# Order of the four products per chunk, and x times v in two halves, in an FFT convolution with an expert layer behind it

## The chip, the cores and the metric

The kernel runs on one core of a Trainium2 chip. The metric is the device time of one execution in microseconds; the time before is a median of three runs. Engines are named as in the profile: PE (TensorE), DVE (VectorE), ACT (ScalarE), POOL (GpSimd), SP (the queue that issues every DMA here).

## The reference

```python
u = x * v                                  # (4, 12480, 128)
L = 2 * S
Uf = np.fft.rfft(u, n=L, axis=1)
Hf = np.fft.rfft(h_filt, n=L, axis=0)      # h_filt: a small MLP of pos_emb, times exp(-0.01 t)
y = np.fft.irfft(Uf * Hf[None], n=L, axis=1)[:, :S, :]
x = x * y                                  # (49920, 128)
h = x @ w_in                               # 2048 wide
out = (h * clip(h + 3, 0, 6) / 6) @ w_out
```

A long convolution of u = x times v with a filter, done by Fourier transforms, gates x; an expert layer with two matrix products follows.

## The kernel before, in words

The transform of length 64 x 196 is split in two stages forth and two stages back, each a set of matrix products with constant tables. The work comes in eight groups of channels. The function `filter` makes the filter's spectrum and the first stage of group 0. Then `period(g)` runs for g = 0 to 7, each with 25 chunks of four of the 99 frequencies. In one period TensorE does, for each chunk, the second stage of group g (L301, `spectra`, for the chunk after the one in hand) and the third stage (L546, `third_stage`, for a chunk three back). In between stand the transposes of group g - 1 (L557, `back`) with its fourth stage (L575), and, in eight visits of each period but the last, the first stage of group g + 1 (L282, `visit`). The output of the convolution goes to device memory. `last_turn` ends the convolution, and the class `Moe` then does the expert layer.

A chunk's way over the engines is this. TensorE puts the second stage into a PSUM bank `s2`, of which there are two. ACT copies it with real and imaginary half exchanged into the bank `sw`, of which there is one: two instructions, L499 and L500 (`swapped`). DVE then makes four products with the filter's spectrum `h`. Two read `s2`: `pq` at L520 and `pa` at L521. Two read `sw`: `pq2` at L522 and `pa2` at L523. POOL adds them up at L527 in three steps: `pq` into half of `pa`, `pq2` into half of `pa2`, and `pa2` into `pa`. (In period 0 the third step of two chunks in three is done by DVE at L533, behind the next chunk's products.) The third stage reads `pa`. L521 is the last reader of `s2`, and L523 the last reader of `sw`; the next second stage but one needs the first, and the next swap the second.

There is no scheduler: each engine takes its instructions in the order in which the functions are called, and waits for the semaphores of what it depends on. In an iteration the call of `chunk` comes first (products, third stage, second stage of the next chunk), then `fourth_stage`, `gate_next`, and then a loop with `back`, `weight` and `visit`. Two or three light chunks follow each other, about 2.5 us of TensorE each, and then a chunk with a visit and a fourth stage, about 8 us; this is called a cycle here.

`gate_next` multiplies x and v for sixteen channels of one piece (L453, on POOL) into a tile `u`, in the chunks of the lists GATES (`1, 4, 8, 11, 14, 17, 20, 22`) and GATES0 (for period 0). Behind it `load_next` issues four DMAs on SP for a later x and v (L442). Each product is made two halves ahead of the visit that reads it. In periods 1 to 6, `weight` puts steps of decoding the expert layer's weights on DVE (L225 to L247), three per call in some chunks, behind the chunk's products; period 7 has no visits.

Of the kernel before, what the change touches and what calls it, by code (L numbers as in the profile page):

```python
# [13 lines left out]
ALU = mybir.AluOpType  # L14
# [23 lines left out]
G = 32  # L38
GB = 2
# [149 lines left out]
def pool(tc, name, bufs=1, **kw):  # L189
    return tc.tile_pool(name=name, bufs=bufs, reuse_waits="tile", **kw)  # L190
# [60 lines left out]
class Conv:  # L251
    def __init__(self, tc, nc, left, right, x, v, c_tab, d_tab, g_tab, ident, hd, yd, weights):
        self.tc, self.nc, self.left, self.right = tc, nc, left, right
        self.x, self.v, self.g_tab, self.ident, self.hd, self.yd = x, v, g_tab, ident, hd, yd
        self.c_tab, self.d_tab, self.weights = c_tab, d_tab, weights
        self.loaded, self.gated, self.n_loaded = [], [], 0
        self.first, self.second, self.pend, self.steps = [], [], [], None
        self.tabs, self.n_tabs, self.hs, self.n_hs = [], 0, [], 0
        self.out, self.sum = None, None
        self.keep = right.enter_context(pool(tc, "keep", side="right"))  # L260
        self.z = [self.keep.tile([128, K2, COLS], F32, name=f"z{i}") for i in range(2)]
        self.dtab = self.keep.tile([K2, 2, 64], F32, name="dtab")
        big = left.enter_context(pool(tc, "big"))
        self.ctab = big.tile([R[0], 2 * K2], F32, name="ctab")
# [181 lines left out]
    def gate_next(self):  # L446

        if self.loaded:
            half, xt, vt, again = self.loaded.pop(0)
            if half == 0:  # L450
                self.gated.append(self.up.tile([R[0], G, N1], F32, tag="u", name="u"))
            u = self.gated[-1][:, half * G // 2 : (half + 1) * G // 2, :]
            self.nc.gpsimd.tensor_tensor(out=u, in0=xt, in1=vt, op=ALU.mult)  # L453
            if again:
                self.load_next()
# [47 lines left out]
    def products(self, item):  # L503

        nc, P = self.nc, 128
        g, c, kw, t, tab = item
        sw = self.swapped(t, kw)
        hs = self.hs.pop(0)
        a = self.pr.tile([P, CH, 2 * GB, G], F32, tag="a", name="pa", bufs=4)
        a2 = self.pr.tile([P, CH, 2 * GB, G], F32, tag="a2", name="pa2")  # L510
        q = self.pr.tile([P, CH, GB, G], F32, tag="q", name="pq")
        q2 = self.pr.tile([P, CH, GB, G], F32, tag="q2", name="pq2")
        uv = t.rearrange("p (k s g) -> p k s g", k=CH, g=G)[:, :kw]
        sv = sw.rearrange("p (k s g) -> p k s g", k=CH, g=G)[:, :kw]

        def h(ci, si, m):
            return hs[:, ci, :kw, si, :].unsqueeze(2).to_broadcast([P, kw, m, G])

        mul, add = ALU.mult, ALU.add
        nc.vector.tensor_tensor(out=q[:, :kw], in0=uv[:, :, :GB], in1=h(0, 1, GB), op=mul)  # L520
        nc.vector.tensor_tensor(out=a[:, :kw], in0=uv, in1=h(0, 0, 2 * GB), op=mul)  # L521
        nc.vector.tensor_tensor(out=q2[:, :kw], in0=sv[:, :, :GB], in1=h(1, 1, GB), op=mul)  # L522
        nc.vector.tensor_tensor(out=a2[:, :kw], in0=sv, in1=h(1, 0, 2 * GB), op=mul)  # L523
        self.load_h()

        def plus(x, y):
            nc.gpsimd.tensor_tensor(out=x, in0=x, in1=y, op=add)  # L527

        plus(a[:, :kw, GB:], q[:, :kw])
        plus(a2[:, :kw, GB:], q2[:, :kw])  # L530
        if self.sum:
            s, s2 = self.sum
            nc.vector.tensor_tensor(out=s, in0=s, in1=s2, op=add)  # L533
        self.sum = None
        if g == 0 and c % 3:
            self.sum = a[:, :kw], a2[:, :kw]
        else:
            plus(a[:, :kw], a2[:, :kw])
        return g, c, kw, tab, a
# [61 lines left out]
    def period(self, g):  # L601


        n = 0
        if g == 1:
            self.ext.close()
            self.dp = self.left.enter_context(pool(self.tc, "dp"))
            self.wp = self.right.enter_context(pool(self.tc, "wp", 2, side="right"))
        for c in range(NCHUNK):
            end = min(32, 32 * (c + 1 - START) // (NCHUNK - 1 - START))  # L610
            self.chunk(g, c)
            if c in (0, NCHUNK - 1):
                self.fourth_stage()
            if c in (GATES if g else GATES0):
                self.gate_next()
            while n < end:
                if g:
                    self.back(g - 1, 4 * n)
                    self.weight(n)
                n += 1  # L620
                if n % VISIT == 0:
                    if g + 1 < NG:
                        self.visit(g + 1, n // VISIT - 1)
                    if n < 28 and g + 1 < NG:
                        self.fourth_stage()
                if n % VISIT == 2 and VISIT < n < 28 and g + 1 == NG:
                    self.fourth_stage()
# [267 lines left out]
```

## Time and profile before

| | us |
|---|---|
| median of 3 runs (3169.38 to 3170.16) | 3170.02 |
| the profiled execution | 3166.51 |
| its span | 3164.7 |
| filter and first stage of group 0 | about 160 |
| period 0 | about 85 |
| periods 1 to 6, each | 107 to 111 |
| period 7, and the last turn | about 87, and 53 |
| expert layer | about 2120 |

A row of the timeline gives the start and length in us, the engine, the line, the operation, the output and inputs by name, the shape, how many instructions were merged, and in brackets the engine's idle time before it with what ended it by the profile. The bank `s2` and the bank of the third stage both appear as `s`. A second or third stage of one chunk is eight TensorE records (six in the last chunk). A row of the waits gives who waited for whom, the total in us, how often, and the longest wait.

### The profile page before, as it was taken

The numbers are of one execution on the slowest core, as the hardware profiler recorded it, in microseconds if no ns is written. First come the engines' busy times: TensorE is split into PE (matmuls) and PEld (weight loads), VectorE is DVE, ScalarE is ACT, GpSimd is POOL, SyncE is SP. The second block draws the span as 40 slices with busy tenths as digits, with TensorE's granted clock in tenths as the row PEclk, the third lists the DMA queues.
The fourth block names the chain that finished last, engine by engine and source line by source line (L and its number), as shares of the span: only waits on it lengthen the run. The fifth ranks groups of instructions, "written<-read, shape, count | busy, mean of one in ns | idle before, by whom it ended". The sixth has DMA issues, their size and how long they took to land.

```text
span 3164.7 us, 53332 instructions
## 1 busy us (share of the span) xinstructions
PE 3114.2 (98%) x19916; PEld 2633.9 (83%) x19916; DVE 2305.8 (73%) x2707; ACT 2351.7 (74%) x3039; POOL 2079.2 (66%) x1240
## 2 busy tenths in 40 slices
PE   9989999999999999999999999999999999999999
PEld 8978888888887788888888888888888888888887
DVE  4467666767654777777777777777777777777776
ACT  2367767767766777878787777777777877777777
POOL 1188777777874666666666666666666666666666
PEclk9999999999999999999999999999999999999999
DMA  6688888787855111111111110111111111111110
GB/s 236 211 205 230 228 230 234 218 238 221 228 172 202 54 36 35 38 42 35 35 40 31 41 41 30 41 39 32 41 36 35 39 32 41 38 33 40 40 31 24
DMA packets 232273, 304.66 MB, mean 96 GB/s; under 512 B 38055, under 2 KB 159310, under 8 KB 231118
## 3 DMA queue, kind: packets, MB, share of 16 engines
q1 hardware_dynamic: 232014, 301.26, 32.6%
q8 instruction: 157, 2.57, 0.3%
q14 instruction: 102, 0.84, 0.1%
HBM read 224.87 MB, written 76.28 MB: 95 GB/s over the span
## 4 chain that ended last, share of the span: by engine, by line
PE 68%; POOL 0%; DVE 0%; ACT 0%; DMA 0%; issue 0%; ACTq 0%
PE acc L827 11%; PE acc L823 11%; PE acc L824 11%; PE ph L788 11%; PE ph L790 11%; PE ph L789 11%; PE ts L575 0%; PE s L557 0%; PE ts L557 0%; POOL pa L527 0%; DMA yd<-y 0%; POOL glo L812 0%; DVE y L596 0%; ACT o L594 0%; ACT ghi L810 0%
## 5 line engine op out<-in xcount | busy, mean ns | idle before, releaser
L812 POOL TENSOR_TENSOR glo<-g,ghi 128x1024 fp32r<-128x1024 f32 x588 | 1404.4, 2397 | 761.2 <-ACT ghi L810 761.0
L800 DVE SCALAR_TENSOR_TENSOR g<-r,ph 128x1024 f32<-128x1024 f32 (+1 forms) x784 | 949.7, 1211 | 408.7 <-ACT r L798 408.3
L798 ACT ACTIVATE r<-ph,three 128x1024 f32<-128x1024 f32 (+1 forms) x784 | 871.1, 1111 | 273.6 <-PE ph L790 273.4
L810 ACT CAST ghi<-g 128x1024 fp32r<-128x1024 f32 (+1 forms) x784 | 811.1, 1035 | 1.9 <-DVE g L800 1.0
L788 PE MATMUL ph<-xhi,win_hi 128*128 128x512 f32 (+1 forms) x1568 | 608.5, 388 | 0.0
L789 PE MATMUL ph<-xlo,win_hi 128*128 128x512 f32 (+1 forms) x1568 | 608.4, 388 | 0.0
L790 PE MATMUL ph<-xhi,win_lo 128*128 128x512 f32 (+1 forms) x1568 | 608.3, 388 | 0.0
L824 PE MATMUL acc<-ghi,wout_lo 128*128 128x512 f32 (+1 forms) x1568 | 608.0, 388 | 0.0
L823 PE MATMUL acc<-ghi,wout_hi 128*128 128x512 f32 (+1 forms) x1568 | 607.9, 388 | 0.0
L827 PE MATMUL acc<-glo,wout_hi 128*128 128x512 f32 (+1 forms) x1568 | 481.3, 388 | 0.6 <-POOL glo L812 0.6
L527 POOL TENSOR_TENSOR pa<-pa,pq 128x256 f32<-128x256 f32 (+1 forms) x400 | 295.6, 747 | 171.3 <-DVE pa L521 133.2
L788 PEld LDWEIGHTS ph<-xhi,win_hi 128*128 128x128 f32 x1568 | 294.4, 188 | 61.5 <-issue 0.8
L827 PEld LDWEIGHTS acc<-glo,wout_hi 128*128 128x128 f32 x1568 | 293.6, 188 | 61.7 <-POOL glo L812 1.5
L824 PEld LDWEIGHTS acc<-ghi,wout_lo 128*128 128x128 f32 x1568 | 294.5, 188 | 60.5
L790 PEld LDWEIGHTS ph<-xhi,win_lo 128*128 128x128 f32 x1568 | 294.4, 188 | 60.5
L823 PEld LDWEIGHTS acc<-ghi,wout_hi 128*128 128x128 f32 x1568 | 294.4, 188 | 60.4
L789 PEld LDWEIGHTS ph<-xlo,win_hi 128*128 128x128 f32 x1568 | 294.5, 188 | 60.4
L812 DVE TENSOR_TENSOR glo<-g,ghi 128x1024 fp32r<-128x1024 f32 x196 | 283.7, 1448 | 0.0
L520 DVE TENSOR_TENSOR pq<-s,h 128x256 f32<-128x256 f32 (+1 forms) x200 | 84.1, 421 | 255.7 <-POOL pa L527 162.2
L761 DVE TENSOR_TENSOR xy<-xt,yt 128x512 f32<-128x512 f32 x96 | 258.7, 2695 | 0.0
L301 PE MATMUL s<-z,tab 128*128 128x128 f32 x1584 | 213.9, 278 | 35.5 <-DVE pa L521 27.9
L527 POOL TENSOR_TENSOR pa<-pa,pa 128x512 f32<-128x512 f32 (+1 forms) x184 | 232.5, 1263 | 14.4
(61 smaller groups left out, 3620.6 us busy)
## 6 DMA issues: line engine op xcount, KB each, us to landing
tab<-in_g_tab SPq DMA_DIRECT2D x192, 256.0 KB
h<-hd SPq DMA_DIRECT2D x384, 128.0 KB
yd<-y SPq DMA_DIRECT2D x64, 512.0 KB
xt<-in_xt SPq DMA_DIRECT2D x98, 256.0 KB
out<-o SPq DMA_DIRECT2D x97, 256.0 KB
xt<-in_x SPq DMA_DIRECT2D x64, 384.0 KB
vt<-in_v SPq DMA_DIRECT2D x64, 384.0 KB
yt<-yd SPq DMA_DIRECT2D x256, 64.0 KB
```

The lines of the kernel that those rows point to most:

```text
L527: nc.gpsimd.tensor_tensor(out=x, in0=x, in1=y, op=add)
L761: self.nc.vector.tensor_tensor(out=xy.rearrange("p (n e c) -> p n e c", e=4, c=GH), in0=xt.rearrange("p (n e c) -> p n e c", e=4, c=GH), i ...
L788: nc.tensor.matmul(ph[:, i, :ne], self.win_hi[:, sl], hi[:, :ne], start=True, stop=False)
L789: nc.tensor.matmul(ph[:, i, :ne], self.win_hi[:, sl], lo[:, :ne], start=False, stop=False)
L790: nc.tensor.matmul(ph[:, i, :ne], self.win_lo[:, sl], hi[:, :ne], start=False, stop=True)
L798: nc.scalar.activation(r[:, :, :ne], ph[:, :, :ne], AF.Relu, bias=self.three)
L800: nc.vector.scalar_tensor_tensor(out=g[:, :, :ne], in0=r[:, :, :ne], scalar=6.0, in1=ph[:, :, :ne], op0=ALU.min, op1=ALU.mult)
L810: nc.scalar.copy(ghi[:, :, :ne], g[:, :, :ne])
L812: e.tensor_tensor(out=glo[:, :, :ne], in0=g[:, :, :ne], in1=ghi[:, :, :ne].bitcast(F32), op=ALU.subtract)
L823: nc.tensor.matmul(a, self.wout_hi[:, f, :], ghi[:, i, :ne], start=(f == 0), stop=False)
L824: nc.tensor.matmul(a, self.wout_lo[:, f, :], ghi[:, i, :ne], start=False, stop=False)
L827: nc.tensor.matmul(a, self.wout_hi[:, f, :], glo[:, i, :ne], start=False, stop=(f == NFC - 1))
```

## The change

Three things are changed. In `products` the two products that read `sw` come before the two that read `s2`, and POOL's first two additions change places in the same way. `gate_next` makes only eight of the sixteen channels; the other eight are made by the new function `gate_rest`, which `period` calls in the next chunk, behind `fourth_stage` and ahead of the next `gate_next`. During `filter` (when `self.ps` is None) both halves are made at once. The loads behind the product, `load_next`, are now issued by `gate_rest`.

```diff
+        self.out, self.sum, self.gating = None, None, None
...
+            c = G // 4
+            self.nc.gpsimd.tensor_tensor(out=u[:, :c], in0=xt[:, :c], in1=vt[:, :c], op=ALU.mult)
+            self.gating = u[:, c:], xt[:, c:], vt[:, c:], again
+            if self.ps is None:
+                self.gate_rest()
+
+    def gate_rest(self):
+
+        if self.gating:
+            u, xt, vt, again = self.gating
+            self.gating = None
             self.nc.gpsimd.tensor_tensor(out=u, in0=xt, in1=vt, op=ALU.mult)
             if again:
                 self.load_next()
...
+        nc.vector.tensor_tensor(out=q2[:, :kw], in0=sv[:, :, :GB], in1=h(1, 1, GB), op=mul)
+        nc.vector.tensor_tensor(out=a2[:, :kw], in0=sv, in1=h(1, 0, 2 * GB), op=mul)
         nc.vector.tensor_tensor(out=q[:, :kw], in0=uv[:, :, :GB], in1=h(0, 1, GB), op=mul)
         nc.vector.tensor_tensor(out=a[:, :kw], in0=uv, in1=h(0, 0, 2 * GB), op=mul)
-        nc.vector.tensor_tensor(out=q2[:, :kw], in0=sv[:, :, :GB], in1=h(1, 1, GB), op=mul)
-        nc.vector.tensor_tensor(out=a2[:, :kw], in0=sv, in1=h(1, 0, 2 * GB), op=mul)
...
+        plus(a2[:, :kw, GB:], q2[:, :kw])
         plus(a[:, :kw, GB:], q[:, :kw])
-        plus(a2[:, :kw, GB:], q2[:, :kw])
...
                 self.fourth_stage()
+            self.gate_rest()
             if c in (GATES if g else GATES0):
```

On TensorE and ACT the instructions stand in the same order as before. On DVE two chunks of a middle period stood like this (`s2`, `sw` and `h` carry a number for each buffer, so that the two chunks can be told apart):

```order
L520 TENSOR_TENSOR pq_5438<-s2_5411,h_5208 128x256
L521 TENSOR_TENSOR pa_5436<-s2_5411,h_5208 128x512
L522 TENSOR_TENSOR pq2_5439<-sw_5433,h_5208 128x256
L523 TENSOR_TENSOR pa2_5437<-sw_5433,h_5208 128x512
L520 TENSOR_TENSOR pq_5522<-s2_5458,h_5257 128x256
```

The same place of the changed program, where the lines are eleven higher:

```order
L531 TENSOR_TENSOR pq2_5463<-sw_5457,h_5237 128x256
L532 TENSOR_TENSOR pa2_5461<-sw_5457,h_5237 128x512
L533 TENSOR_TENSOR pq_5462<-s2_5441,h_5237 128x256
L534 TENSOR_TENSOR pa_5460<-s2_5441,h_5237 128x512
L531 TENSOR_TENSOR pq2_5554<-sw_5548,h_5280 128x256
```

The last reader of `s2` was the second of four and is now the fourth; the last reader of `sw` was the fourth and is now the second. Nothing else on DVE has moved.

On POOL, behind the sums of a chunk in whose iteration `gate_next` is called, with the whole sums of the chunk after it:

```order
L527 TENSOR_TENSOR pa_4622<-pa_4622,pa2_4623 128x512
L453 TENSOR_TENSOR u_4654<-xt_4303,vt_4304 98x1024
L527 TENSOR_TENSOR pa_4675<-pa_4675,pq_4677 128x4x64
L527 TENSOR_TENSOR pa2_4676<-pa2_4676,pq2_4678 128x4x64
L527 TENSOR_TENSOR pa_4675<-pa_4675,pa2_4676 128x512
```

The same place in the changed program:

```order
L538 TENSOR_TENSOR pa_4648<-pa_4648,pa2_4649 128x512
L454 TENSOR_TENSOR u_4680<-xt_4367,vt_4368 98x512
L538 TENSOR_TENSOR pa2_4696<-pa2_4696,pq2_4698 128x4x64
L538 TENSOR_TENSOR pa_4695<-pa_4695,pq_4697 128x4x64
L538 TENSOR_TENSOR pa_4695<-pa_4695,pa2_4696 128x512
L464 TENSOR_TENSOR u_4680<-xt_4367,vt_4368 98x512
```

One product of 1024 elements a row stood between two chunks' sums; now half of it stands there and the other half behind the next chunk's sums. On SP the four loads of x and v follow the second half: they have moved behind the two `h` loads and the table load of one more chunk.

More of the change, by code (lines that the diff above doesn't have):

```diff
@@ L258, in __init__ @@
         self.tabs, self.n_tabs, self.hs, self.n_hs = [], 0, [], 0
-        self.out, self.sum = None, None
+        self.out, self.sum, self.gating = None, None, None
         self.keep = right.enter_context(pool(tc, "keep", side="right"))
```

## The prediction

> **What bounds the kernel now.** I read first the page, then the busy time by stage, then the waits, and last the timeline of single chunks. The convolution ends near 1045 us and the expert layer behind it is not touched, so only the eight periods count.
>
> ```profile
> PE 3114.2 (98%) x19916; PEld 2633.9 (83%) x19916; DVE 2305.8 (73%) x2707; ACT 2351.7 (74%) x3039; POOL 2079.2 (66%) x1240
> ```
>
> The table by stretch has one row for period 0, one for a typical middle period, and those of periods 6 and 7 (columns: length, then busy us of PE, PEld, DVE, ACT, POOL, then clock, DMA share, GB/s).
>
> ```profile
> 160.00:245.00 85.00, 72.33 (x892) 67.70 (x890) 60.18 (x116) 53.44 (x105) 71.21 (x67) 0.98 0.88 214
> 465.00:576.00 111.00, 107.75 (x1102) 94.35 (x1100) 78.97 (x150) 79.10 (x151) 86.34 (x84) 0.98 0.82 228
> 798.00:905.00 107.00, 105.65 (x1102) 92.99 (x1100) 64.29 (x127) 78.42 (x149) 81.19 (x81) 1.00 0.72 205
> 905.00:992.00 87.00, 84.45 (x590) 70.48 (x587) 57.80 (x116) 62.11 (x116) 67.43 (x75) 1.00 0.66 211
> ```
>
> In a middle period TensorE is busy 107.75 of 111.00 us, and POOL, the next, 86.34: TensorE sets the length, and anything that makes it wait is paid in full. Only period 0 has room, 12.67 us. The waits say what it waits for:
>
> ```profile
> ACT sw L499 <- DVE pa L523: 97.3, 85, 2.6
> DVE pq L520 <- ACT sw L500: 28.6, 26, 2.5
> PE s L301 <- DVE pa L521: 27.9, 21, 2.1
> ```
>
> So ScalarE waits 85 times for the one bank of the swapped spectrum, which L523 frees, and TensorE waits 21 times for one of the two banks of the second stage, which L521 frees. The change frees the first earlier and the second later. The question is which of the two is on TensorE's path.
>
> One cycle of period 3 from the timeline (chunks 5, 6, 7; then the first-stage work of a visit follows):
>
> ```profile
> 484.17 1.06 PE L301 MATMUL s<-z,tab 128*128 128x128 f32 x8
> 485.07 0.84 PE L557 MATMUL ts<-ident,z 128*99 128x128 f32 x4
> 485.94 0.59 ACT L560 COPY w<-ts 99x512 f32<-99x512 f32 x1 [0.98 <-PE ts L557]
> 486.56 0.56 ACT L499 COPY sw<-s 64x512 f32<-64x512 f32 x1
> 486.64 1.06 PE L301 MATMUL s<-z,tab 128*128 128x128 f32 x8
> 487.14 0.57 ACT L500 ACTIVATE sw<-s 64x512 f32<-64x512 f32 x1
> 487.80 0.42 DVE L520 TENSOR_TENSOR pq<-s,h 128x256 f32<-128x256 f32 x1 [1.33 <-POOL pa L527]
> 488.14 0.68 DVE L521 TENSOR_TENSOR pa<-s,h 128x512 f32<-128x512 f32 x1
> 488.74 0.42 DVE L522 TENSOR_TENSOR pq<-sw,h 128x256 f32<-128x256 f32 x1
> 489.07 0.68 DVE L523 TENSOR_TENSOR pa<-sw,h 128x512 f32<-128x512 f32 x1
> 489.10 1.11 PE L301 MATMUL s<-z,tab 128*128 128x128 f32 x8
> 489.84 0.56 ACT L499 COPY sw<-s 64x512 f32<-64x512 f32 x1 [0.85 <-DVE pa L523]
> ```
>
> Read it backwards. The second stage of chunk 7 (489.10) takes the bank that chunk 5 filled at 484.17, and L521 of chunk 5 ended at 488.14 + 0.68 = 488.82: 0.28 us to spare, wake-up included. VectorE had started at 487.80 because the swap ended at 487.14 + 0.57 = 487.71 (the row names POOL, but the swap is what ended just before). The swap started at 486.56, behind the copy L560 that ended at 486.53, which waited for L557 on TensorE. The previous chunk's L523 is not in this chain. That chain hangs on TensorE alone from end to end.
>
> **The order of the four products.** Today L521 ends 488.82 - 487.80 = 1.02 us after VectorE starts a chunk, and L523 at 489.75, 0.93 us later. With the order turned round the swapped bank is free after about 1.02 us and the second-stage bank after 1.95. VectorE's start moves neither way in this place: before as after, its first product stands behind the whole swap. So chunk 5's bank comes 0.93 us later, and of the 0.28 us to spare a part is wake-up. How much, this pair shows, where TensorE did stall (chunk 20's L521, the second stage of chunk 22):
>
> ```profile
> 556.22 0.68 DVE L521 TENSOR_TENSOR pa<-s,h 128x512 f32<-128x512 f32 x1
> 557.15 0.68 DVE L523 TENSOR_TENSOR pa<-sw,h 128x512 f32<-128x512 f32 x1
> 557.16 1.02 PE L301 MATMUL s<-z,tab 128*128 128x128 f32 x7 [2.06 <-DVE pa L521]
> ```
>
> 556.22 + 0.68 = 556.90, and TensorE starts at 557.16: 0.26 us. The other end is ScalarE's wake-up in the cycle above, 0.09 us (L523's end at 489.75 to L499 at 489.84). So the cover at chunk 5 is between 0.02 and 0.19 us, and the stall between 0.74 and 0.91; I take 0.84, nearer to TensorE's own pair. Where TensorE stalls already, as at chunk 20, the whole 0.93 is added. The one tight place with real cover is chunk 11:
>
> ```profile
> 513.96 0.68 DVE L521 TENSOR_TENSOR pa<-s,h 128x512 f32<-128x512 f32 x1
> 515.60 1.06 PE L301 MATMUL s<-z,tab 128*128 128x128 f32 x8
> ```
>
> It ends at 514.64, 0.96 us ahead of its taker, and pays 0.06 to 0.23: I take 0.15.
>
> A period has eight visits, so eight cycles. Counting period 3 chunk by chunk in the timeline: chunks 2, 14, 20 and 22 stall already (4 x 0.93 = 3.72), 5, 8 and 17 stand at the edge like the one shown (3 x 0.84 = 2.52), 11 pays 0.15, and 19's stall is swallowed by 20's, which hangs on VectorE's queue. Sum 6.4 us. In the heavy part after each cycle VectorE and ScalarE run dry and start afresh from TensorE, so nothing carries over and nothing is given back. Periods 1 to 5 have the same places: 5 x 6.4 = 32.0. Period 6 has no decoding: one place with 0.93, five with 0.84, 11's 0.15, and 0.10 for 19 and 20 together (there the earlier swap pays for the later bank), 5.4. Period 7 has no visits; three places like chunk 5 (2.5), and in the others the earlier swap makes up for it: 2.4 with a little off at its end.
>
> **Period 0.** Here the swapped bank is on the path. One cycle of three chunks:
>
> ```profile
> 199.85 1.13 PE L301 MATMUL s<-z,tab 128*128 128x128 f32 x8 [1.39 <-DVE pa L521]
> 205.62 0.42 DVE L520 TENSOR_TENSOR pq<-s,h 128x256 f32<-128x256 f32 x1 [1.03 <-ACT sw L500]
> 207.68 0.56 ACT L499 COPY sw<-s 64x512 f32<-64x512 f32 x1 [1.59 <-DVE pa L523]
> 208.27 0.57 ACT L500 ACTIVATE sw<-s 64x512 f32<-64x512 f32 x1
> 208.87 0.42 DVE L520 TENSOR_TENSOR pq<-s,h 128x256 f32<-128x256 f32 x1 [1.30 <-ACT sw L500]
> 209.22 0.68 DVE L521 TENSOR_TENSOR pa<-s,h 128x512 f32<-128x512 f32 x1
> ```
>
> TensorE's next second stage, which takes the bank that L521 frees at 209.90, closes the cycle. With the change: products start at 205.62, the swapped bank is free at 206.64, the next swap starts 0.11 later as it does now (206.75), takes 1.16 (207.68 to 208.84), products start at 207.94, and the second-stage bank is free 1.95 later, at 209.89. That is the same to 0.01 us: what the swap gains the bank gives back. I take 0, with -2 to +2 for the first chunks.
>
> **The two half products of x and v, and the loads.** GpSimd's prices by shape:
>
> ```profile
> L527 POOL TENSOR_TENSOR pa<-pa,pq 128x256 f32<-128x256 f32 x384 | 285.9, 753 | 168.8 <-DVE pa L521 131.1 <-PE s L546 13.2 <-issue 7.2
> L527 POOL TENSOR_TENSOR pa<-pa,pa 128x512 f32<-128x512 f32 x176 | 224.5, 1276 | 13.8
> L453 POOL TENSOR_TENSOR u<-xt,vt 98x1024 f32<-98x1024 f32 x64 | 152.6, 2386 | 133.2 <-PE ts L282 91.9 <-DMA vt<-in_v 39.9 <-POOL u L453 1.5
> ```
>
> A half should take about 1276 ns, so two cost 2552 in place of 2386: 64 x 0.17 = 11 us more on GpSimd. It hides in GpSimd's idle time, 24.66 us in a middle period, as long as the sums come early enough for the third stage:
>
> ```profile
> 494.30 1.27 POOL L527 TENSOR_TENSOR pa<-pa,pa 128x512 f32<-128x512 f32 x1
> 501.82 1.06 PE L546 MATMUL s<-pa,tab 128*128 128x128 f32 x8
> 205.94 1.27 POOL L527 TENSOR_TENSOR pa<-pa,pa 128x512 f32<-128x512 f32 x1
> 207.71 1.06 PE L546 MATMUL s<-pa,tab 128*128 128x128 f32 x8
> ```
>
> Chunk 6's sum is ready at 495.57, 6.25 us ahead; in period 0 the shortest is 207.21, 0.50 ahead, and there the half in front of it is 1.1 us shorter than today's whole. So the split brings and costs nothing: 0. If the cover went in period 0 it would be 0.17 x 9 = 1.5 us. The first stage takes u two halves later, so a rest that comes a chunk later is still early. The four loads of the next x and v go into SP's queue a chunk later, behind that chunk's two h loads and its table; they serve the second next product of a half, about two visits away, so nobody waits: 0.
>
> What takes a little back: short pauses in TensorE's queue, 0.09 us a cycle, behind copies that do not shift with it, some -1.5 in all.
>
> **The sum.** 32.0 + 5.4 + 2.4 + 0 + 0 - 1.5 = +38.3 us. On the profiled execution, 3166.51 us, that makes 3204.8; the median of the runs is 3170.02, 3.5 above it, so the timed median should be 3170.0 + 38 = 3208.
>
> [...] Of the decoding steps on VectorE, one has this row (shortest, median and longest in ns):
>
> ```profile
> L225 DVE TENSOR_SCALAR dec<-raw x16: 283/1202/1434, 267.7 to 822.5; 128x256 int32<-128x256 int32 x16
> ```
>
> The same instruction takes 283 ns or up to 1434. [...]
>
> **The rivals.**
> [...] Chance 0.12.
> *The swapped bank was the real brake.* For it: 97.3 us of waiting, 85 times, against 27.9 for the other bank. If the products start 0.93 us sooner wherever they also free the second-stage bank, the middle periods pay nothing, period 0 gains 0.93 in each of seven cycles (6.5) and period 7 some 3: 3170 - 10 = 3160. It decides if the swap at the edge places waits for L523 and not for L560. Against it: 486.56 follows 486.53. Chance 0.10.
> *Cover everywhere.* The bank is late but TensorE's queue has pauses enough: 3170 within 6. Against it: the 3.25 us idle in the middle period are already these waits. Chance 0.05.
> *GpSimd falls behind,* or products and swap, which now run side by side, slow each other by 0.1 us each in 175 chunks: 12 us more, 3220. For it only that no row shows the two together. Chance 0.06.
> The forecast has the remaining 0.67.
>
> **How the numbers follow.** Forecast's own ends: 5 x (6.0 to 6.7) + (4.9 to 5.8) + (1.5 to 3.2) + (-2 to +2) + (-3 to 0), so 31 to 45: 3201 to 3215. The range must also take in the first rival and part of the last: 3186 to 3218. A measurement here tells 0.2% (6 us) from no change. Faster by more: the second rival, 0.10; within: 0.05; slower: 0.85.
>
> **What would show it.** In the changed profile a middle period should be 117 us long instead of 111, with TensorE's wait for the last product of the second-stage bank grown from 27.9 to some 65 us, at chunks 2, 5, 8, 14, 17, 20 and 22; ScalarE's wait for the swapped bank should fall from 97.3 us to a few; period 0 should stay at 85. The forecast is wrong if middle periods keep 111 us, or if the products of chunk 5 start earlier against TensorE's second stage than 487.80 - 484.17 = 3.63 us.

## The result, and the profile after

Timed, the changed kernel takes 3206.85 us (3205.13 to 3209.16, four runs) against 3169.70 us for the kernel before (four runs): the ratio is 1.0117, with a 95% interval of 1.0101 to 1.0133. It is slower by about 37 us. Its profiled execution took 3205.13 us with a span of 3203.3, 38.6 more than that of before. The first line of its page:

```profile
PE 3118.5 (97%) x19916; PEld 2633.0 (82%) x19916; DVE 2301.4 (72%) x2707; ACT 2366.1 (74%) x3039; POOL 2092.6 (65%) x1304
```

The work is the same; only GpSimd has 64 more instructions. TensorE's busy time grew by 4.3 us, the span by nine times as much, so the rest is waiting. The table by stretch, for period 0, period 3, period 6 and period 7 of the changed kernel (columns as in the prediction; the stretches begin 1.5 to 2 us after the period's first second stage):

```profile
160.90:245.50 84.60, 71.65 (x889) 67.27 (x888) 60.85 (x114) 54.64 (x104) 72.83 (x74) 0.98 0.84 212
476.20:592.50 116.30, 107.08 (x1102) 93.42 (x1104) 77.76 (x150) 80.76 (x151) 87.88 (x92) 1.00 0.75 218
826.50:939.30 112.80, 107.16 (x1102) 93.51 (x1104) 64.73 (x128) 80.27 (x149) 82.35 (x88) 1.00 0.65 191
939.30:1033.00 93.70, 87.35 (x602) 72.31 (x600) 57.88 (x118) 65.10 (x117) 68.83 (x78) 1.00 0.65 209
```

Period 0 kept its length to within 0.7 us. Period 3 has 116.30 us where it had 111, with TensorE's busy time no longer than before (107.08): its idle time went from 3.25 to 9.22 us. The group of second-stage matmuls before and after, with the idle time of TensorE ahead of them behind the second bar, and three rows of the waits after:

```profile
L301 PE MATMUL s<-z,tab 128*128 128x128 f32 x1584 | 213.9, 278 | 35.5 <-DVE pa L521 27.9 <-issue 3.5 <-ACT raw L243 2.3
L301 PE MATMUL s<-z,tab 128*128 128x128 f32 x1584 | 216.2, 279 | 71.4 <-ACT sw L510 35.2 <-DVE pa L534 20.6 <-DMA yd<-y 9.8
PE s L301 <- ACT sw L510: 35.2, 43, 1.6
PE s L301 <- DVE pa L534: 20.6, 17, 2.6
ACT sw L510 <- DVE pa L532: 24.4, 29, 1.7
```

In the kernel before that group had 35.5 us of idle time ahead of it (27.9 of it put down to the second-stage bank). Now it has 71.4: 35.9 more, nearly the whole 38.6. The name behind the arrow has to be read with care. It is the last event that the profile saw, and in the cycle below it is wrong: the row there names a decoding step, which has nothing to do with the bank. In the timeline it is the end of L534, the bank's last reader, that stands just ahead of TensorE's start (0.25 us there, 0.11 us ahead of chunk 24's second stage, whose row names the swap). ScalarE's wait for the swapped bank fell from 97.3 to 24.4 us, and the kernel was none the faster for it.

The lengths of the periods in the timelines of the two kernels, from each period's first second-stage matmul to the next one's (period 7 to the last third stage of the convolution):

| | before | after | difference | predicted |
|---|---|---|---|---|
| filter and first stage of group 0 | 158.6 | 159.4 | 0.8 | 0 |
| period 0 | 83.9 | 84.6 | 0.7 | 0 |
| period 1 | 109.3 | 113.9 | 4.6 | 6.4 |
| periods 2, 3, 4 | 111.0, 110.9, 110.9 | 116.3 each | 5.3, 5.4, 5.4 | 6.4 each |
| period 5 | 110.9 | 117.7 | 6.8 | 6.4 |
| period 6 | 107.1 | 112.7 | 5.6 | 5.4 |
| period 7 | 91.3 | 95.0 | 3.7 | 2.4 |

**The cycle at chunk 5.** The timeline of the changed kernel, period 3, at the place that the prediction worked through:

```profile
496.42 1.06 PE L301 MATMUL s<-z,tab 128*128 128x128 f32 x8
498.19 0.59 ACT L571 COPY w<-ts 99x512 f32<-99x512 f32 x1 [0.99 <-PE ts L568]
498.80 0.56 ACT L510 COPY sw<-s 64x512 f32<-64x512 f32 x1
499.39 0.57 ACT L511 ACTIVATE sw<-s 64x512 f32<-64x512 f32 x1
500.05 0.42 DVE L531 TENSOR_TENSOR pq<-sw,h 128x256 f32<-128x256 f32 x1 [1.33 <-POOL pa L538]
501.32 0.68 DVE L534 TENSOR_TENSOR pa<-s,h 128x512 f32<-128x512 f32 x1
502.25 0.46 PE L301 MATMUL s<-z,tab 128*128 128x128 f32 x2 [0.74 <-DVE dec L225]
```

The products start 500.05 - 496.42 = 3.63 us after the second stage, to the hundredth as before, since the swap still stands behind the copy of `w`. L534 lets the bank go at 502.00; TensorE starts at 502.25, and the row's own releaser, a decoding step, is only the instruction that ran next on VectorE. The two second stages are 5.83 us apart; they were 4.93. That is 0.90 us more for this place.

**Period 0.** The end of the cycle that the prediction shows for the kernel before, and one cycle after the change:

```profile
210.15 1.02 PE L301 MATMUL s<-z,tab 128*128 128x128 f32 x7 [1.39 <-DVE pa L521]
```

```profile
200.66 1.13 PE L301 MATMUL s<-z,tab 128*128 128x128 f32 x8 [0.46 <-DVE pa L534]
206.41 0.42 DVE L531 TENSOR_TENSOR pq<-sw,h 128x256 f32<-128x256 f32 x1 [2.96 <-ACT sw L511]
208.74 0.42 DVE L531 TENSOR_TENSOR pq<-sw,h 128x256 f32<-128x256 f32 x1 [0.38 <-ACT sw L511]
210.01 0.68 DVE L534 TENSOR_TENSOR pa<-s,h 128x512 f32<-128x512 f32 x1
210.94 1.13 PE L301 MATMUL s<-z,tab 128*128 128x128 f32 x8 [0.46 <-DVE pa L534]
```

From one chunk's products to the next one's it is 2.33 us now, and was 3.25 (205.62 to 208.87): here the earlier swap does bring its 0.92. The bank, freed by the last product instead of the second, gives it back: the cycle is 210.94 - 200.66 = 10.28 us long, and was 210.15 - 199.85 = 10.30.

### The profile page after: what moved, and what is told of

It reads as the page before. It is cut to its first block, busy times and chain, and to the rows that moved or that the text cites. A ratio compares the mean times of both kernels' runs of the same rounds, so it can differ in the third digit from the quotient of the medians.

```text
span 3203.3 us, 53489 instructions
## 1 busy us (share of the span) xinstructions
PE 3118.5 (97%) x19916; PEld 2633.0 (82%) x19916; DVE 2301.4 (72%) x2707; ACT 2366.1 (74%) x3039; POOL 2092.6 (65%) x1304
## 4 chain that ended last, share of the span: by engine, by line
PE 72%; ACT 1%; DVE 0%; DMA 0%; POOL 0%; issue 0%; SPq 0%; DVEq 0%; ACTq 0%; POOLq 0%
PE acc L839 11%; PE acc L836 11%; PE acc L835 11%; PE ph L800 11%; PE ph L801 11%; PE ph L802 11%; PE ts L568 2%; PE ts L586 1%; PE s L301 1%; PE ts L282 1%; PE s L557 1%; DMA yd<-y 0%; PE s L568 0%; ACT w L571 0%; ACT sw L510 0%
## 5 line engine op out<-in xcount | busy, mean ns | idle before, releaser
L531 DVE TENSOR_TENSOR pq<-sw,h 128x256 f32<-128x256 f32 (+1 forms) x200 | 83.8, 419 | 290.1 <-POOL pa L538 143.1
L301 PE MATMUL s<-z,tab 128*128 128x128 f32 x1584 | 216.2, 279 | 71.4 <-ACT sw L510 35.2
L301 PEld LDWEIGHTS s<-z,tab 128*128 128x128 f32 x1584 | 193.3, 192 | 83.9 <-ACT sw L510 81.7
```

The source lines that it names most:

```text
L301: self.nc.tensor.matmul(t[:, i * 128 : (i + 1) * 128], tab[:, i, :], z[:, c * CH + i, :], start=True, stop=True)
```

## The experiments

**1 and 2. The parts of the change alone.** In the first kernel only the order of the products and sums is changed, in the second only the split with the later loads.

```diff
+        nc.vector.tensor_tensor(out=q2[:, :kw], in0=sv[:, :, :GB], in1=h(1, 1, GB), op=mul)
+        nc.vector.tensor_tensor(out=a2[:, :kw], in0=sv, in1=h(1, 0, 2 * GB), op=mul)
         nc.vector.tensor_tensor(out=q[:, :kw], in0=uv[:, :, :GB], in1=h(0, 1, GB), op=mul)
         nc.vector.tensor_tensor(out=a[:, :kw], in0=uv, in1=h(0, 0, 2 * GB), op=mul)
-        nc.vector.tensor_tensor(out=q2[:, :kw], in0=sv[:, :, :GB], in1=h(1, 1, GB), op=mul)
-        nc.vector.tensor_tensor(out=a2[:, :kw], in0=sv, in1=h(1, 0, 2 * GB), op=mul)
...
+        plus(a2[:, :kw, GB:], q2[:, :kw])
         plus(a[:, :kw, GB:], q[:, :kw])
-        plus(a2[:, :kw, GB:], q2[:, :kw])
```

The second kernel has the rest of the change and not these lines.

> The order of the four products (and of GpSimd's first two sums) is changed, the product of x and v stays whole. Theory (the second-stage bank is held 0.93 us longer): all of the loss is here, 3206 us, within 4, and TensorE's period 3 is 116 us long. Rival (the halves and the later loads make GpSimd or SP late): 3170, or in between if both have a share.

Measured: 3203.62 us against 3170.38, ratio 1.0106 (1.0092 to 1.0119). The order alone costs 33 us.

> Only the product of x and v is split; the products keep the order of before. Theory: 3170 us within 3, all periods as before, GpSimd 11 to 14 us busier in all. Rival (late sums or loads cost): over 3176. Rival in favour (VectorE's decoding is held off for shorter): under 3165.

Measured: 3175.03 us, ratio 1.0016 (1.0007 to 1.0025). A miss: the split, which was to cost nothing, costs 4.7 us. 33 and 4.7 make up about the 37 of the whole change. Two places in the second kernel's trace show new waits. In period 1 TensorE stands once for a table of the second stage, a wait that neither the kernel before nor the whole change has anywhere:

```profile
256.85 0.91 PE L301 MATMUL s<-z,tab 128*128 128x128 f32 x6 [1.94 <-DMA tab<-in_g_tab]
```

And chunk 10's second stage comes 0.42 to 0.65 us later against its neighbours in each of periods 1 to 6, 2.8 us together. It takes the bank of chunk 8. The cause stands further up VectorE's queue: a decoding step behind chunk 6's products (L231). First that step in the kernel before, and the start of chunk 8's products there; then GpSimd's second half of u (L464), the step beside it, and the start of chunk 8's products, with the split (period 4 in both):

```profile
604.16 0.41 DVE L231 SCALAR_TENSOR_TENSOR dec<-dec 128x256 int32<-128x256 int32 x1
612.34 0.42 DVE L520 TENSOR_TENSOR pq<-s,h 128x256 f32<-128x256 f32 x1
```

```profile
608.91 1.29 POOL L464 TENSOR_TENSOR u<-xt,vt 98x512 f32<-98x512 f32 x1
609.87 1.30 DVE L231 SCALAR_TENSOR_TENSOR dec<-dec 128x256 int32<-128x256 int32 x1
618.94 0.42 DVE L531 TENSOR_TENSOR pq<-s,h 128x256 f32<-128x256 f32 x1
```

The step takes 1.30 us in place of 0.41, and what follows in the queue comes later. Chunk 9's second stage starts at 610.50 in the kernel before and at 616.46 here, so chunk 8's products stand 1.84 us behind it and then 2.48. TensorE had about 0.2 us to spare and pays the rest.

**3 and 4. A third bank for the second stage.** If the late release of that bank is all of the loss, a third bank takes it away. So that the banks stay eight in all, the third stage gives up one of its two. The first kernel is the changed one with it, the second the kernel before.

```diff
-    BANKS = {"s2": 2, "sw": 1, "s3": 2, "ts": 3}
+    BANKS = {"s2": 3, "sw": 1, "s3": 1, "ts": 3}
```

> The changed kernel with three second-stage banks and one third-stage bank in place of two and two. Theory: the longer hold costs nothing once a third bank is there, so TensorE's waits for the last product go, the swap's shorter loop is left as a gain (period 0 under 80 us), and one third-stage bank costs some tenths of a us in the light chunks: 3145 us, 3125 to 3172. Rival (swap and products side by side slow each other, or the halves cost): stays over 3190, as the bank had no part in it.

> The kernel before with three second-stage banks and one third-stage bank. Theory: TensorE's 14 us of waits for L521 in periods 1 to 7 go, period 0 keeps its length as there the swap's one bank paces the chunks, the single third-stage bank takes some back: 3160 us, 3150 to 3178, and slower than the changed kernel with the same banks by 5 to 25 us. Rival (order does not matter beside the banks): the two are equal within 3 us.

Measured: the changed order takes 3162.43 us (ratio to the kernel before 0.9971, 0.9959 to 0.9983), the old order 3182.28 (1.0033, 1.0021 to 1.0045). TensorE's waits from 160 to 1040 us, first with the new order, then with the old:

```profile
PE s L557 <- ACT z L561: 9.4, 22, 1.4
PE s L301 <- DMA tab<-in_g_tab: 8.0, 11, 1.7
PE ts L282 <- ACT w L571: 6.1, 10, 0.8
PE s L301 <- DVE pa L534: 2.0, 2, 1.7
```

```profile
PE s L546 <- ACT z L550: 21.8, 36, 1.9
PE ts L282 <- ACT w L560: 13.8, 21, 1.1
PE s L301 <- DVE pa L521: 0.8, 1, 0.8
```

The wait for the second-stage bank is gone from both but for 2.0 and 0.8 us. What is left is the third stage's single bank, which the copy `z` on ScalarE frees, and `w`, also ScalarE's; with the new order also 8.0 us put down to the loads of the second stage's tables. With the old order ScalarE still waits 98.8 us for the swapped bank in this stretch, with the new order 41.7; its copies come later, and TensorE waits 35.6 us for them against 15.5. So the other half of the idea is true: with three banks the order is worth 20 us (3182.28 to 3162.43). How much of that goes by the copies was not tried apart. The old order's 3182 was a miss: I had it gain from the third bank. So was period 0 with the new order: it was to fall under 80 us and took 83.2.

**5. Half the lateness.** A third order of the products: `a2, q, a, q2`. The second-stage bank is freed by the third product (1.62 us after VectorE starts, 0.60 later than before), the swapped bank by the fourth, as before.

```diff
+        nc.vector.tensor_tensor(out=a2[:, :kw], in0=sv, in1=h(1, 0, 2 * GB), op=mul)
         nc.vector.tensor_tensor(out=q[:, :kw], in0=uv[:, :, :GB], in1=h(0, 1, GB), op=mul)
         nc.vector.tensor_tensor(out=a[:, :kw], in0=uv, in1=h(0, 0, 2 * GB), op=mul)
         nc.vector.tensor_tensor(out=q2[:, :kw], in0=sv[:, :, :GB], in1=h(1, 1, GB), op=mul)
-        nc.vector.tensor_tensor(out=a2[:, :kw], in0=sv, in1=h(1, 0, 2 * GB), op=mul)
```

> The kernel before with the products in the order pa2, pq, pa, pq2: the second-stage bank comes free 0.6 us later than before, the swapped bank as late as before. Theory (the price is the hold of the second-stage bank): two thirds of the loss in periods 1 to 6, some 3.3 us each, and, as no earlier swap pays for it, a longer period 0 (85 to 90 us): 3197 us, 3188 to 3204. Rival (the loss comes from swaps that run beside the products, because their bank is free sooner): 3170, as that bank is not free sooner here.

Measured: 3212.75 us, ratio 1.0133 (1.0116 to 1.0149), slower than the whole change and above the range. Period 0 did what was expected of it:

```profile
161.40:250.90 89.50, 72.53 (x886) 68.14 (x887) 69.69 (x111) 53.62 (x102) 70.05 (x65) 0.96 0.80 197
```

5.6 us longer than before: there the lateness is paid at every cycle, since no earlier swap makes up for it. The middle periods are 5.6 us longer too, where 0.60/0.93 of the change's 5.4 would be 3.5. Their timelines show 0.4 to 0.7 us at seven places, and 1.66 us at one, where a decoding step has met GpSimd's whole product:

```profile
509.51 2.37 POOL L453 TENSOR_TENSOR u<-xt,vt 98x1024 f32<-98x1024 f32 x1
511.36 2.04 DVE L225 TENSOR_SCALAR dec<-raw 128x256 int32<-128x256 int32 x1
```

In the kernel before the same step of the same period started 0.10 us ahead of that product's end:

```profile
487.40 2.37 POOL L453 TENSOR_TENSOR u<-xt,vt 98x1024 f32<-98x1024 f32 x1
489.67 0.28 DVE L225 TENSOR_SCALAR dec<-raw 128x256 int32<-128x256 int32 x1
```

0.28 or 2.04 us for one instruction, which against GpSimd's product starts 0.42 us earlier in experiment 5: 0.52 us ahead of the product's end, and it outlasts the product by 1.52 us, beside the sums that follow it on GpSimd (1.42 us from 511.83 on). What ties the two instructions together the traces do not show. Whether the decoding is the whole excess is tried below.

**6. The new order with three banks, without the split.**

> The new order of the products with the whole product of x and v, three second-stage banks and one third-stage bank. Theory: what the split alone costs (5 us) goes off the 3162 us of the changed kernel with these banks: 3158 us, 3153 to 3163. Rival (with three banks GpSimd's sums are what TensorE waits for, and the split helps them): over 3163.

Measured: 3162.65 us, ratio 0.9974 (0.9964 to 0.9985): the same as with the split (3162.43). That is inside the range, but the 5 us that were to go off are not there: with these banks the split's cost is not seen.

**7 and 8. What of the split costs.** One kernel makes both halves at once, so that only GpSimd's time is longer; the other keeps the whole product and only issues the loads a chunk later. Both have the products in the old order. Their edits against the changed kernel, without that of the order:

```diff
-            if self.ps is None:
-                self.gate_rest()
+            self.gate_rest()
```

```diff
-            c = G // 4
-            self.nc.gpsimd.tensor_tensor(out=u[:, :c], in0=xt[:, :c], in1=vt[:, :c], op=ALU.mult)
-            self.gating = u[:, c:], xt[:, c:], vt[:, c:], again
+            self.nc.gpsimd.tensor_tensor(out=u, in0=xt, in1=vt, op=ALU.mult)
+            self.gating = (again,)
...
-            u, xt, vt, again = self.gating
+            again = self.gating[0]
             self.gating = None
-            self.nc.gpsimd.tensor_tensor(out=u, in0=xt, in1=vt, op=ALU.mult)
```

> The product of x and v in two halves, both made at once, the loads where they were; products in the order of before. If the split's 5 us come from the place of the second half and of the loads: 3170 within 2. If they come from the longer time on GpSimd: 3174 or more.

> The product of x and v whole and where it was, but the next loads of x and v issued a chunk later, as in the change. If the split's 5 us come from the loads, which then stand in SP's queue ahead of other tables: 3173 to 3176, with a wait of TensorE for a table. If they come from the halves on GpSimd: 3170 within 2.

Measured: 3169.83 us (0.9999, 0.9990 to 1.0008) and 3169.22 us (0.9997, 0.9988 to 1.0006). Neither costs anything. The kernel with the later loads has no wait for a table either, so the loads' place alone doesn't make that wait. What is left of the split is the place of the second half, behind the next chunk's sums, alone or together with the loads. The traces bear this out: the decoding step L231 of experiment 2 behind chunk 6's products takes 0.41 us in both of these kernels, as in the kernel before, against 1.29 to 1.31 in all six periods of experiment 2. Of the 4.7 us, 2.8 are those of chunk 10's place; the table's wait, 1.94 us long, was seen once in one execution, and what it costs in the others is open.

**9, 10 and 11. Without decoding.** Is the loss carried by the decoding steps, as experiment 5 suggests? Three kernels without them: the old order, the whole change, and the order of experiment 5.

```diff
-            self.steps = decode(self.nc, raw, buf[:, : 2 * NW], buf[:, 2 * NW :])
+            self.steps = blank(self.nc, raw)
```

> The kernel before with the eleven decoding steps of the weights left out (one write of zeros stands for them, so the expert layer's output is not the reference's, its work is the same). Both theories: the long wait at chunk 22 and the one at chunk 4 shrink, periods 1 to 5 are near period 6's 107 us: 3150 us, 3145 to 3156. This is the base for the next two.

> The changed kernel without the decoding steps (as in the run before). Theory (the hold alone sets the loss, decoding only moves some of it): 38 us over the kernel before without decoding, 33 to 44, some 5.6 in each of periods 1 to 6. Rival (much of the loss is that decoding steps meet GpSimd's instructions at a worse time): under 25 us.

> The order pa2, pq, pa, pq2 without the decoding steps. Theory (price by the length of the hold, 0.6 us in place of 0.93, plus period 0, which no earlier swap repays; what this order cost beyond that came from decoding steps caught behind GpSimd's whole product): 29 us over the kernel before without decoding, 24 to 33, and below the changed kernel without decoding. Rival (the price does not go with the hold): at or over the changed kernel, as with decoding.

Measured: 3151.16, 3189.07 and 3176.91 us, all three inside their ranges. The change costs 37.9 us without any decoding, as much as with it. The third order costs 25.8 us, and is now below the whole change; its excess in experiment 5 was the decoding. The second-stage group in the three traces, in the same order (the lines are seven higher in these kernels, and L528, L541 and L529 are the bank's last readers):

```profile
L308 PE MATMUL s<-z,tab 128*128 128x128 f32 x1584 | 214.0, 278 | 24.7 <-DVE pa L528 18.5 <-DMA h<-hd 3.6 <-DVE pq L529 1.8
```

```profile
L308 PE MATMUL s<-z,tab 128*128 128x128 f32 x1584 | 217.4, 281 | 53.5 <-ACT sw L517 24.4 <-DVE pa L541 15.5 <-DMA yd<-y 9.9
```

```profile
L308 PE MATMUL s<-z,tab 128*128 128x128 f32 x1584 | 215.9, 279 | 44.0 <-DVE pa L529 29.3 <-issue 11.9 <-DMA yd<-y 1.3
```

Idle time ahead of the second stage rises by 28.8 us where the bank is 0.93 us late and by 19.3 where it is 0.60 late: 0.67 of it, for 0.65 of the lateness. The times rise in the ratio 25.8 to 37.9, 0.68. The price goes with the time for which the bank is held. One thing has to be kept apart: the third order also pays 4.1 us in period 0, where the whole change pays 0.6. In periods 1 to 6 alone it is 18.9 against 31.2 us, 0.61. (The whole change has the split in it besides; its cost without decoding was not tried alone.)

**12. What the third stage's bank was worth.** The kernel before with two banks for the second stage and one for the third, seven in all.

```diff
-    BANKS = {"s2": 2, "sw": 1, "s3": 2, "ts": 3}
+    BANKS = {"s2": 2, "sw": 1, "s3": 1, "ts": 3}
```

> The kernel before with one third-stage bank in place of two, and still two second-stage banks: what the bank given away costs by itself. Theory: TensorE's third stage waits for ScalarE's copy, 15 to 30 us: 3185 to 3200 us. With that, the third second-stage bank would have brought the old order 5 to 15 us and the new order 55 or more. Rival: under 3175, the bank is free to give.

Measured: 3184.08 us, ratio 1.0045 (1.0029 to 1.0062). Giving up that bank costs 13 us, a little less than the 15 to 30 expected. With the third second-stage bank the old order lost 12 (experiment 4), so that bank brings it about 1 us back, less than these runs scatter and not the 5 to 15 that I had expected. If the 13 hold for the new order too, which was not tried, the third bank is worth some 57 us there (44 from 3206.85 to 3162.43, and the 13).

## Why the prediction was right, point by point

**The bank and not the swap is on TensorE's path: right.** Experiment 1 has 33 of the 37 us in the order alone; with a third bank the loss is gone; and without decoding the loss scales with the time the bank is held. The rival that the swapped bank was the real brake fell for this kernel, and is true of the same kernel with three banks: there the order gains 20 us. That products and swap slow each other where they now run side by side is not borne out: at chunk 5 they take 0.42 and 0.68, 0.56 and 0.57 us as before.

**Period 0 comes out even: right.** The cycle is 10.28 us long for 10.30, as predicted at 0.93 gained against 0.93 lost. Experiment 5 shows the loss without the gain: 5.6 us.

**The middle periods: the mechanism right, the term too large.** Periods 1 to 5 were to cost 32.0 us and cost 27.5 (1.4 of it a slower clock in period 5, see the end), and 24.8 in the kernel of experiment 1. Place by place in period 3, from the shifts of the second stages between the two timelines:

| chunk whose bank is late | predicted | measured |
|---|---|---|
| 2 | 0.93 | 0.93 |
| 5 | 0.84 | 0.91 |
| 8 | 0.84 | 0.58 |
| 11, with small pauses near it | 0.15 | 0.21 |
| 14 | 0.93 | 0.98 |
| 17 | 0.84 | 0.75 |
| 19 to 21 | 0.93 | 1.07 |
| 22 | 0.93 | 0.16 |
| end of the period | 0 | -0.24 |

The step that failed is "chunks 2, 14, 20 and 22 stall already (4 x 0.93 = 3.72)", at chunk 22. Between the products of chunk 20 and those of chunk 22 VectorE has only its own queue of products and decoding steps. Their first instructions in the kernel before, and in that of experiment 1, which has the new order alone:

```profile
555.89 0.42 DVE L520 TENSOR_TENSOR pq<-s,h 128x256 f32<-128x256 f32 x1
566.38 0.42 DVE L520 TENSOR_TENSOR pq<-s,h 128x256 f32<-128x256 f32 x1
```

```profile
572.14 0.42 DVE L520 TENSOR_TENSOR pq<-sw,h 128x256 f32<-128x256 f32 x1
582.64 0.42 DVE L520 TENSOR_TENSOR pq<-sw,h 128x256 f32<-128x256 f32 x1
```

10.49 us before, 10.50 after, with 0.14 us of VectorE's idle time in either. Both banks come 0.93 us late against the same queue; TensorE has paid for the first, and the second finds it already that much later: chunk 22's place costs 0.01 us in experiment 1. Without decoding (experiments 9 and 10) VectorE stands idle between the two chunks, and chunk 22 pays 0.75 us of its own. The prediction says this of 19 and 20 in one sentence and doesn't apply it to 20 and 22. In the kernel with the whole change the stretch is 10.64 us long, but by another way: three decoding steps in it are 2.2 us shorter together, VectorE then waits 1.12 us for a decoding step on ScalarE, and the step behind that wait takes 1.52 us instead of 0.41,

```profile
580.47 1.52 DVE L245 TENSOR_TENSOR dec<-dec,raw 128x256 f32<-128x256 f32 x1 [1.12 <-ACT raw L243]
```

so that its 0.16 is near experiment 1's 0.01 in part by chance. At chunk 8 it was the cover: there the products stood behind a decoding step that is 0.15 us shorter after, and TensorE had 0.21 us of room.

**Period 6 and period 7.** 5.6 us against 5.4, though spread otherwise (0.7 at chunks 19 and 20, where 0.10 was predicted, and less elsewhere). The prediction says that this period has no decoding; in fact it has 11 of the 33 steps of the others, among them those around chunk 8. Period 7 cost 3.7 against 2.4: six places paid 0.58 to 0.91 where three were counted, and the end took 1.1 back. "In the others the earlier swap makes up for it" held for too few.

**The split at nothing: wrong, 4.7 us.** The step that failed is that its cover was looked for only at the third stage, GpSimd's taker. The traces show the loss on VectorE: beside the second half in its new place a decoding step takes 1.30 us in place of 0.41, and chunk 8's bank comes later for it. With the order changed as well that queue has room: in experiment 1 VectorE stands 0.40 us at chunk 7's products for the swap and 0.40 us ahead of L245 for ScalarE. There the split makes periods 2 to 4 only 0.2 to 0.3 us longer (116.3 against 116.0 to 116.1); what more it costs in the whole change stays open. The lower end of the range, 3186, took in a first rival, by which the split would make the decoding shorter; no run shows a gain from that. The split alone was slower by the 4.7 us; in the changed kernel the decoding steps take 116.6 us of VectorE in all, for 122.0 before, and no period is shorter for it.

**The small pauses, -1.5: not found** at 0.09 us a cycle; the pauses of 0.07 us that the timelines show add to the loss, and 0.24 us comes back at the end of a middle period.

**The sum.** On the medians the order's term was 5 us too large (38.3, pauses included, against 33) and the split's 4.7 too small: that the sum came within 1.2 us is luck, those two errors cancelling. One price of a rival does not come out of its own numbers: 0.1 us in each of 175 chunks is 17.5 us, not 12.

**What was to be seen.** Middle periods of 116.3 for 117; the wait for the second-stage bank, read as the idle time of its group, 71.4 instead of 65; products at chunk 5 at 3.63 us. ScalarE's wait for the swapped bank, 24.4 us, was to be "a few", a miss.

## What to carry to other kernels

Putting one reader of a buffer ahead of another moves two releases, one sooner and one later. Follow each back to the engine that sets the length: a wait of 97 us on an engine with time to spare is worth less than one of 28 on the engine without. Where two stalls of that engine hang on one queue of another, a delay of that queue is paid once, not twice (0.01 us at chunk 22 in experiment 1, behind chunk 20). And when the order is to be changed, change the number of buffers with it: the same order that lost 33 us gained 8 over the kernel before with one bank moved from the third stage to the second, a move that cost the old order 12.

## What the runs showed of the hardware

The table by stretch of the kernel before shows TensorE's granted clock drop behind a stall, and that of the changed kernel at the same chunk does not (the visit behind chunk 20's bank):

```profile
556.00:559.00 3.00, 1.84 (x12) 1.70 (x12) 2.93 (x7) 0.77 (x2) 1.73 (x3) 0.87 0.63 225
559.00:562.00 3.00, 3.00 (x40) 2.89 (x41) 3.00 (x5) 1.88 (x5) 3.00 (x2) 0.56 0.54 153
562.00:565.00 3.00, 3.00 (x44) 2.87 (x41) 2.97 (x4) 2.23 (x5) 2.92 (x4) 1.00 0.50 149
```

```profile
575.00:577.00 2.00, 2.00 (x36) 1.88 (x37) 2.00 (x3) 0.98 (x2) 2.00 (x2) 1.00 0.71 192
```

In the kernel before a stall of 2.06 us was followed by stretches at 0.87 and 0.56 of the clock, and the visit took 4.17 us instead of 2.96. Periods 1, 3 and 5 of that kernel have such a visit (4.17 to 4.25 us, at a clock of 0.68 to 0.70), each behind a stall of 2.06 us; periods 2 and 4 have stalls of 2.09 and 2.06 us at the same place, and visits of 2.96. In the changed kernel a stall of 2.24 us at this place left the clock at 1.00. The one slow visit of its periods 1 to 5 (4.24 us, at 0.68) stands at the end of period 5, behind chunk 22's bank and a stall of 1.55 us, and is why that period is 1.4 us longer than its neighbours. So the length of the stall alone doesn't decide: 2.06 us was followed by the slow clock in period 3 and not in period 4. What else decides, these runs do not show. In the kernel before the slow visit cost next to nothing, since the wait for chunk 22's bank behind it was shorter by as much: the two second stages that follow start 2.61 us apart in periods 1, 3 and 5, and 4.02 and 4.04 in periods 2 and 4.
